# Weight rows in three padded runs, and new planning constants, in a top-k attention and two-MLP kernel

## The chip, the cores and the metric

The kernel runs on one core of a Trainium2 chip. The metric is the device time of one execution in microseconds; the runs of before are 702.24, 703.14 and 704.08 us, median 703.14.

## What is computed

Attention over 2 batches, 8 heads, 576 positions of 64, in which each row keeps its 32 largest scores; the result goes as 1152 tokens of 512 through a leaky MLP of width 2048 and then through a gated product MLP of width 1536.

```python
scores = scale * np.matmul(q, k.transpose(0, 1, 3, 2))
kth = np.partition(scores, -top_k, axis=-1)[..., -top_k:-top_k + 1]
scores = np.where(scores >= kth, scores, -1000000000.0)
attn = np.exp(scores - max); attn = attn / (sum + 1e-09)
x = (attn @ v) as 1152 x 512
...
h = x @ w_in
x = (np.maximum(h, 0.0) + alpha * np.minimum(h, 0.0)) @ w_out
...
return (x @ w_a) * (x @ w_b) @ w_out2
```

The weights are handed in as 64-bit words; in each the kernel finds one 32-bit float spread over a low and a high half.

## The kernel before

**Conversion.** The five weights (wi, wo, wa, wb, w2) are 68 blocks of 128 partitions by 512 words. `to_f32` makes floats of one block: SyncE loads it into a buffer `raw` of six (`RAWB`), ScalarE makes two 16-bit halves of a correction `rlo` (L195, L196), VectorE shifts the high halves left by 3 into the block's place in `wi_sb`, `wo_sb`, `wa_sb`, `wb_sb` or `w2s` (L197: it reads every second 32-bit word), and GpSimd adds the correction in place (L198). After each second block `square` sums its squares on TensorE (L208) and VectorE (L210). w2 is stored to HBM in between and loaded again.

**Attention.** 72 tiles of 128 rows in six groups. `front` makes scores on TensorE (L435), `middle` finds the top 32 on VectorE by four MAX8 (L446, L455) and three MATCH_REPLACE (L453), and forms the masked exponentials (L462); it has eight steps k = 0 to 7. `norm` closes a tile with a reciprocal (L469) and a scaling on GpSimd (L470). `back` transposes: for batch 0 on TensorE at step `KBACK`, for batch 1 ("lifted", the last 36 tiles) by a transposing DMA on SyncE's queue (L488) at step `KLIFT`. `av` multiplies with V (L527, L522). `fetch` runs `FA` tiles ahead.

**The MLPs.** `moe1` and `moe2` run group by group in the order `ORDER`; the first three groups' products take the weights as converted, the later ones as two 16-bit halves that `pair` makes in the background. `l1` and `l3` are matmuls (L610, L614), `l2` and `l4` (L622, L625) add up the outputs. `finish` hands the output of `moe1` to `moe2`: a square sum on ScalarE, three small scale steps on VectorE (`pow2`, L115 to L117), the rescaling into two halves (L695 on ScalarE, L696 on VectorE), transposes (L700) and a copy to `xT` (L701).

**What sets the order.** Three tracks are written out by the loop at the end: `dve` (attention and conversion: 26 blocks mixed with the first eight tiles, then 42 blocks, then the tiles), `mlp`, and `bg` (the pairs). The track whose planned clock plus shift is lowest goes next; `SHIFT_ATT` is taken off the clock of `dve`, `SHIFT_BG` is added to that of `bg`, `T_PAIR` is what a pair is planned at. This gives a priority to each instruction, and at build time a scheduler sets the order on each engine by it; `tc.high_priority(offset=...)` moves the instructions in it ahead, by `HPM` for the activations in the MLPs and by `HPY` for `finish`. On the chip each engine then runs its instructions in that order.

Of the kernel before, what the change touches and what calls it, by code (L numbers as in the profile page):

```python
# [20 lines left out]
B, H, S, D = 2, 8, 576, 64
DM = H * D
# [6 lines left out]
NEG = -3.0e38  # L29

LIFT = 2.0 ** 14
KLIFT = 4
KNORM = 0
KAV = 2
KV = 6
# [2 lines left out]
RLOB = 3  # L38
W2B = 3
# [17 lines left out]
STAGES = [(k, g if isinstance(g, tuple) else (g,)) + NATIVE.get((k, g), (1, 1)) for k, g in ORDER]  # L57
DVE = [('open', 0), ('mix', 26, 8), ('xs', 0), ('conv', 42), ('att', 80)]
RAWB = 6
FA = 5  # L60
QA = 1
VA = 0
GTM = 'mdd'
M2M = 'ppd'
F0 = 1
HPY = 0
HPM = 400
SB = 2
KBACK = 3
KFRONT = 1  # L70
SHIFT_ATT = 2.0
SHIFT_BG = 4.0
T_PAIR = 4.0
T_ATT = 5.8
T_CONV = 1.1
F_PE = 1.1

STEPS = 9
CONV = [(n, i) for i in range(NF1) for n in ("wi", "wo")] + [(n, i) for j in range(0, NF2, 2) for n in ("wa", "wb", "w2") for i in (j, j + 1)]
PASSES = ((0, 0), (0, 1), (1, 0))  # L80
# [6 lines left out]
def tile_topk_attention_moe(ctx: ExitStack, tc: tile.TileContext, qT, kT, vM, vL, wi, wo, al, wa, wb, w2, out):  # L87
# [54 lines left out]
    vpart = small("vpart", 8)  # L142

    def square_v(v, b, hp):
        sq = early.tile([P, DM], I32, tag="rlo", name="vsq", bufs=RLOB).bitcast(BF16)[:, 0:5 * P]
        i = 4 * b + hp
        nc.scalar.activation(sq, v.rearrange("p c n -> p (c n)"), AF.Square, accum_out=vpart[:, i:i + 1])

    def x_scale():
        for hp in range(4):  # L150
            v = early.tile([P, DM], I64, tag="raw", name="v_raw", bufs=RAWB).bitcast(F32)[:, 0:5 * P]
            v = v.rearrange("p (c n) -> p c n", c=5)
            load_v(v, 1, hp)
            square_v(v, 1, hp)
            yield
        big = small("vbig", 2)
        row_max(big[:, 0:1], vpart)
        nc.vector.tensor_scalar(big[:, 1:2], big[:, 0:1], 8.0, None, op0=ALU.mult)
        pow2(big[:, 1:2], vsc[:, 0:1], vsc[:, 1:2], 1)
        sq = early.tile([P, NF1], F32, tag="asq", name="asq", bufs=1)  # L160
        nc.vector.tensor_mul(sq, alpha, alpha)
        row_max(amax, sq)
        nc.vector.tensor_scalar(amax, amax, 1.0, None, op0=ALU.max)
        yield


    wsb, wsc, winv, parts = {}, {}, {}, {}
    for name in ("wi", "wo", "wa", "wb"):
        wsb[name] = cp.tile([P, NBLK[name], DM], F32, tag=f"{name}_sb", name=f"{name}_sb")
    all_parts = small("parts", sum(NPART.values()))  # L170
    k0 = 0
    for name, nb in NBLK.items():
# [5 lines left out]
    w2_st = tc.dram_tile([NF2, P, DM], F32, name="w2_st")  # L178
    w2_pr = tc.dram_tile([NF2, P, 2 * DM], F16, name="w2_pr")

    def w2_tile():
        return sp.tile([P, DM], F32, tag="w2s", name="w2s", bufs=W2B)
    srcs = {"wi": wi, "wo": wo, "wa": wa, "wb": wb, "w2": w2}
    w2_tiles = {}

    def to_f32(dst, name, i):
        raw = early.tile([P, DM], I64, tag="raw", name="raw", bufs=RAWB)
        nc.sync.dma_start(raw, srcs[name][i])  # L190
        lo = raw.bitcast(U32).rearrange("p (n t) -> p n t", t=2)[:, :, 0]
        hi = raw.bitcast(I32).rearrange("p (n t) -> p n t", t=2)[:, :, 1]
        d = dst.bitcast(I32)
        r = early.tile([P, DM], I32, tag="rlo", name="rlo", bufs=RLOB)
        nc.scalar.activation(r.bitcast(I16).rearrange("p (n t) -> p n t", t=2)[:, :, 0], lo, AF.Copy, scale=2.0 ** -29)  # L195
        nc.scalar.activation(r.bitcast(BF16).rearrange("p (n t) -> p n t", t=2)[:, :, 1], hi.bitcast(F32), AF.Sign)  # L196
        nc.vector.tensor_scalar(d, hi, 3, None, op0=ALU.logical_shift_left)  # L197
        nc.gpsimd.tensor_tensor(out=d, in0=d, in1=r, op=ALU.add)  # L198

# [11 lines left out]

    def block(name, i):
        if name == "w2":
            t = w2_tile()
            to_f32(t, name, i)
            nc.sync.dma_start(w2_st[i], t)
            held.append(t)
        else:  # L220
            to_f32(wsb[name][:, i], name, i)
            held.append(wsb[name][:, i])
        if i % 2:
            square(name, i // 2, held[-2:] if name == "w2" else [wsb[name][:, i - 1], wsb[name][:, i]])
# [740 lines left out]
def _layout(inputs):  # L965
    import numpy as np

    c = np.ascontiguousarray
    v = inputs["v"].transpose(0, 2, 1, 3).reshape(B, S, DM)

    def rows(w, n):
        return c(w.reshape(n, P, DM)).view(np.int64)

    def columns(w, n):
        return c(w.reshape(4, P, n, P).transpose(2, 1, 0, 3).reshape(n, P, DM)).view(np.int64)

# [28 lines left out]
```

## Time and profile before

| | before |
|---|---|
| median of 3 runs | 703.14 us |
| span of the profiled execution, first to last instruction | 698.3 us |
| TensorE busy | 611.0 us |
| VectorE busy | 557.5 us |
| ScalarE busy | 482.2 us |
| GpSimd busy | 440.6 us |
| mean granted TensorE clock (1 is full speed) | 0.966 |

The profile is one execution; the time of that execution as a whole isn't given, and the median of the runs lies 4.8 us above its span. Busy times are sums over the span; engines work beside each other, so the sums don't add up to a time. What a stretch is limited by is read from the engine that has no idle time in it, and from what the idle engines wait for.

### The profile page before, as it was taken

The page shows a single profiled execution, that of the slowest core. Times are in us where ns is not written, and L with a number is a line of the kernel's source. Part 1 is how long each engine was busy: PE and PEld are TensorE (multiplying, and loading weights), DVE is VectorE, ACT ScalarE, POOL GpSimd, SP SyncE. Part 2 cuts the span into 40 slices and gives each one's busy share as a digit, 9 for nine tenths or more (in the row PEclk, how much of TensorE's full clock was granted, in tenths as well). Part 3 has the DMA queues.
Part 4 walks back from the last instruction along what each step waited for, and adds up shares of the span by engine and source line. Part 5 has one row for each costly group of instructions (what it writes and reads, how often), then busy time and mean ns, then how long its engine had stood idle before and what let it go on. Part 6 is the DMA issues. An engine that isn't in the chain of part 4 may idle for free.

```text
span 698.3 us, 14902 instructions
## 1 busy us (share of the span) xinstructions
PE 611.0 (87%) x5094; PEld 452.6 (65%) x5094; DVE 557.5 (80%) x1340; ACT 482.2 (69%) x1051; POOL 440.6 (63%) x648
## 2 busy tenths in 40 slices
PE   2465579999999898989968799998899999999997
PEld 1344357678766676767648667765777766677775
DVE  3999999769999979889989879999999998320021
ACT  5886999887889987889878635556656655543232
POOL 5875699886656667879988645655566555223221
PEclk9998668999999999999989999999999999999999
DMA  5996799994420132232287665332245421002243
GB/s 163 313 326 202 249 383 310 322 320 146 126 85 27 35 100 67 88 99 62 59 199 181 185 149 134 93 59 46 63 100 123 129 51 36 18 2 58 64 136 107
DMA packets 98492, 94.57 MB, mean 135 GB/s; under 512 B 50416, under 2 KB 72688, under 8 KB 98416
## 3 DMA queue, kind: packets, MB, share of 16 engines
q1 hardware_dynamic: 97104, 91.26, 45.8%
q10 hardware_dynamic: 1312, 2.36, 0.9%
q8 instruction: 40, 0.66, 0.4%
q14 instruction: 36, 0.29, 0.1%
HBM read 74.33 MB, written 8.65 MB: 119 GB/s over the span
## 4 chain that ended last, share of the span: by engine, by line
PE 53%; DVE 16%; DMA 10%; POOL 7%; issue 6%; ACT 6%; SPq 1%; POOLq 0%; ACTq 0%; DVEq 0%
PE hab L610 12%; PE h L610 9%; PE o L622 7%; PE y L622 6%; DVE wk L453 4%; DMA pt<-e 4%; PE ps L435 4%; DVE m L455 4%; PE o L625 2%; PE ha L614 2%; PE hb L614 2%; PE o L527 2%; PE y L625 2%; DVE e L462 2%; PE o L522 2%
## 5 line engine op out<-in xcount | busy, mean ns | idle before, releaser
L455 DVE MAX8 m<-wk 128x8 f32<-128x576 f32 x216 | 162.6, 753 | 2.5
L601 POOL TENSOR_TENSOR gp<-gt,gp 128x256 f16<-128x256 f32 (+1 forms) x112 | 67.5, 611 | 72.9 <-ACT gp L600 63.9
L453 DVE MATCH_REPLACE8 wk<-m,wk 128x576 f32<-128x576 f32 x144 | 106.8, 742 | 0.0
L610 PE MATMUL h<-xT,wi_sb 128*128 128x256 f16 (+1 forms) x960 | 94.8, 251 | 2.6 <-DVE gt L651 1.6
L610 PEld LDWEIGHTS <-wi_sb 128*128 128x128 f16 x960 | 78.8, 98 | 20.5 <-issue 7.6
L622 PEld LDWEIGHTS <-gp 128*128 128x128 f16 x588 | 54.6, 98 | 57.5 <-issue 6.2
L470 POOL TENSOR_SCALAR e<-e,sm 128x576 f32<-128x576 f32 x72 | 54.2, 753 | 51.8 <-DVE sm L469 47.4
L622 PE MATMUL y<-wo_sb,gp 128*128 128x512 f16 x336 | 82.6, 380 | 1.6 <-POOL gp L601 1.5
L435 PE MATMUL ps<-ks,qh 128*128 128x288 f32 x160 | 48.6, 387 | 28.4 <-DVE e L462 19.3
L610 PE MATMUL hab<-xT,wa_sb 128*128 128x256 f16 (+1 forms) x648 | 66.6, 249 | 3.9 <-ACT xT L701 2.0
L622 PE MATMUL o<-w2s,gp 128*128 128x512 f16 x252 | 63.9, 385 | 2.7 <-DMA w2s<-w_pr 2.5
L610 PE MATMUL hab<-xT,wb_sb 128*128 128x256 f16 (+1 forms) x648 | 66.3, 249 | 0.0
L600 ACT ACTIVATE gp<-gt 128x256 f16<-128x256 f32 (+1 forms) x112 | 42.4, 387 | 33.4 <-DVE gt L783 14.4
L446 DVE MAX8 m<-s 128x8 f32<-128x576 f32 x72 | 54.1, 751 | 12.8 <-ACT s L438 9.4
L610 PEld LDWEIGHTS <-wa_sb 128*128 128x128 f16 x648 | 52.9, 98 | 16.7 <-issue 4.2
L462 DVE SCALAR_TENSOR_TENSOR e<-s,m,ep 128x576 f32<-128x576 f32 x72 | 58.2, 808 | 6.4 <-ACT ep L459 1.5
L783 DVE SCALAR_TENSOR_TENSOR gt<-hab,wb_inv,r 128x256 f32<-128x256 f32 (+1 forms) x36 | 15.6, 434 | 59.6 <-ACT r L777 58.3
L610 PEld LDWEIGHTS <-wb_sb 128*128 128x128 f16 x648 | 52.0, 98 | 5.6 <-issue 0.2
L435 PEld LDWEIGHTS ps<-ks,qh 128*128 128x128 f32 x160 | 29.1, 212 | 40.9 <-DVE e L462 18.4
L459 ACT ACTIVATE ep<-s,nb 128x576 f32<-128x576 f32 x72 | 53.9, 749 | 1.5
L195 ACT ACTIVATE rlo<-raw 128x512 int16<-128x512 uint32 x68 | 53.4, 785 | 2.0 <-DMA raw<-in_wi_dram 1.2
L453 DVE MATCH_REPLACE8 wk<-m,s 128x576 f32<-128x576 f32 x72 | 53.4, 742 | 0.0
(204 smaller groups left out, 1422.6 us busy)
## 6 DMA issues: line engine op xcount, KB each, us to landing
w2s<-w_pr SPq DMA_DIRECT2D x48, 256.0 KB, 2.8
w2s<-w_st SPq DMA_DIRECT2D x36, 256.0 KB, 2.8
raw<-in_wi_dram SPq DMA_DIRECT2D x16, 512.0 KB, 5.4
raw<-in_wo_dram SPq DMA_DIRECT2D x16, 512.0 KB, 6.4
raw<-in_wa_dram SPq DMA_DIRECT2D x12, 512.0 KB, 6.0
raw<-in_wb_dram SPq DMA_DIRECT2D x12, 512.0 KB, 5.8
raw<-in_w_dram SPq DMA_DIRECT2D x12, 512.0 KB, 5.1
kr<-in_kT_dram SPq DMA_DIRECT2D x32, 144.0 KB, 2.9
```

Source lines behind the costliest of these rows:

```text
L195: nc.scalar.activation(r.bitcast(I16).rearrange("p (n t) -> p n t", t=2)[:, :, 0], lo, AF.Copy, scale=2.0 ** -29)
L435: nc.tensor.matmul(ps[:, f, 0:HALF], q[:, h % 2, :], ks[h][:, f * HALF:(f + 1) * HALF], start=i == 0, stop=i == len(mm) - 1)
L446: nc.vector.max(m8[:, 0:8], s)
L453: nc.vector.match_replace(out=wk, in_to_replace=m8[:, 8 * r - 8:8 * r], in_values=src, imm_value=NEG)
L455: nc.vector.max(m8[:, 8 * r:8 * r + 8], wk)
L459: nc.scalar.activation(ep, w2(s), AF.Exp, bias=nb, scale=0.125)
L462: nc.vector.scalar_tensor_tensor(w2(e), w2(s), m8[:, 31:32], ep, op0=ALU.is_ge, op1=ALU.mult, accum_out=sm[:, 0:1])
L470: nc.gpsimd.tensor_scalar(e, e, sm[:, 1:2], LIFT if tl["lift"] else 1.0, op0=ALU.mult, op1=ALU.mult)
L600: nc.scalar.activation(h[:, 0:n], t[:, 0:n], AF.Copy)
L601: nc.gpsimd.tensor_sub(l[:, 0:n], t[:, 0:n], h[:, 0:n])
L610: nc.tensor.matmul(dst[:, 0:n], w[a][:, c * P:(c + 1) * P], x[:, b, c, 0:n], start=k == 0, stop=k == 11)
L622: nc.tensor.matmul(dst, act[b][:, s], w[a], start=i == 0 and k == 0, stop=i == last and k == 2)
```

## The change

On the host each row of 512 words becomes three runs of 171 words (513 with one word of padding), each followed by one word of gap, so a row is 516 words. The buffer `raw` has that shape. The two ScalarE passes and the shift read 3 x 171 words of it; the places that the shift writes are one run of 513, so that each block's last word falls on the first word of the next block, which that block's own shift writes later, or on a word that is added at the end of the weight's buffer. GpSimd's add takes 512 words as before. The planning constants are new.

```diff
-KLIFT = 4
+KLIFT = 6
...
-FA = 5
+FA = 6
...
-HPY = 0
-HPM = 400
+HPY = 400
+HPM = 100
 SB = 2
-KBACK = 3
+KBACK = 2
 KFRONT = 1
-SHIFT_ATT = 2.0
-SHIFT_BG = 4.0
-T_PAIR = 4.0
+SHIFT_ATT = 3.0
+SHIFT_BG = 0.0
+T_PAIR = 5.0
...
+RUN = 171
...
-        wsb[name] = cp.tile([P, NBLK[name], DM], F32, tag=f"{name}_sb", name=f"{name}_sb")
+        wrow[name] = cp.tile([P, NBLK[name] * DM + 1], F32, tag=f"{name}_sb", name=f"{name}_sb")
+        wsb[name] = wrow[name][:, 0:NBLK[name] * DM].rearrange("p (i n) -> p i n", n=DM)
...
     def to_f32(dst, name, i):
-        raw = early.tile([P, DM], I64, tag="raw", name="raw", bufs=RAWB)
+        raw = early.tile([P, 3, RUN + 1], I64, tag="raw", name="raw", bufs=RAWB)
         nc.sync.dma_start(raw, srcs[name][i])
-        lo = raw.bitcast(U32).rearrange("p (n t) -> p n t", t=2)[:, :, 0]
-        hi = raw.bitcast(I32).rearrange("p (n t) -> p n t", t=2)[:, :, 1]
+        lo = raw.bitcast(U32).rearrange("p a (n t) -> p a n t", t=2)[:, :, 0:RUN, 0]
+        hi = raw.bitcast(I32).rearrange("p a (n t) -> p a n t", t=2)[:, :, 0:RUN, 1]
         d = dst.bitcast(I32)
-        r = early.tile([P, DM], I32, tag="rlo", name="rlo", bufs=RLOB)
+        r = early.tile([P, 3 * RUN], I32, tag="rlo", name="rlo", bufs=RLOB)
...
-        nc.vector.tensor_scalar(d, hi, 3, None, op0=ALU.logical_shift_left)
-        nc.gpsimd.tensor_tensor(out=d, in0=d, in1=r, op=ALU.add)
+        nc.vector.tensor_scalar(d.rearrange("p (a n) -> p a n", a=3), hi, 3, None, op0=ALU.logical_shift_left)
+        nc.gpsimd.tensor_tensor(out=d[:, 0:DM], in0=d[:, 0:DM], in1=r[:, 0:DM], op=ALU.add)
...
-            to_f32(wsb[name][:, i], name, i)
+            to_f32(wrow[name][:, i * DM:(i + 1) * DM + 1], name, i)
...
+    def runs(w):
+        w = np.pad(w, ((0, 0), (0, 0), (0, 3 * RUN - DM))).reshape(len(w), P, 3, RUN)
+        return c(np.pad(w, ((0, 0), (0, 0), (0, 0), (0, 1)))).view(np.int64)
```

In the built program the shift's source is 3 runs of 171 and its destination one run of 513; the load is one run of 516 words a partition.

The order on VectorE, from the ninth tile's L462 to its reciprocal, before (`m_860` and `m_1880` are the ninth and tenth tile's maxima in the program's numbering; L115, L137 and L158 are small steps of the scales of V and alpha):

```order
L462 SCALAR_TENSOR_TENSOR e,sm<-s,m_860,ep 128x576
L158 TENSOR_SCALAR vbig<-vbig 128x1
L453 MATCH_REPLACE wk<-m_1880,s 128x576
L210 SCALAR_TENSOR_TENSOR junk,parts<-gram,ident 128x128
L197 TENSOR_SCALAR wo_sb<-raw 128x512
L137 COPY amax<-rmb 128x1
L115 TENSOR_SCALAR e_947<-vbig 128x1
L455 MAX m_1880<-wk 128x8
L197 TENSOR_SCALAR wa_sb<-raw 128x512
L469 RECIPROCAL sm<-sm 128x1
```

The same place in the changed kernel, the last rows up to the ninth reciprocal (its lines are numbered a little higher: L202 is the shift, L468 the masked exponential, L475 the reciprocal; `m_1887` is the tenth tile's):

```order
L202 TENSOR_SCALAR wb_sb<-raw 128x513
L459 MATCH_REPLACE wk<-m_860,wk 128x576
L215 SCALAR_TENSOR_TENSOR junk,parts<-gram,ident 128x128
L202 TENSOR_SCALAR wb_sb<-raw 128x513
L461 MAX m_860<-wk 128x8
L202 TENSOR_SCALAR w2s<-raw 128x513
L468 SCALAR_TENSOR_TENSOR e,sm<-s,m_860,ep 128x576
L459 MATCH_REPLACE wk<-m_1887,s 128x576
L202 TENSOR_SCALAR w2s<-raw 128x513
L461 MAX m_1887<-wk 128x8
L202 TENSOR_SCALAR wa_sb<-raw 128x513
L475 RECIPROCAL sm<-sm 128x1
```

In the piece of before two shifts (the `TENSOR_SCALAR` into `wo_sb`, `wa_sb`) stand ahead of the ninth reciprocal, in that of the changed kernel five; counted from the start 33 against 39 stand ahead of it, at the tenth 40 against 43, at the eleventh 43 against 49, at the twelfth 63 against 64, and all 68 at the fourteenth in both.

The order on VectorE at the changeover from `moe1` to `moe2` of the fourth group, before (`ysq` are the scales, `yb` the rescaled output; the rows into `m_6617` and `m_6738` are attention's):

```order
L117 TENSOR_SCALAR ysq<-e_6868 128x1
L116 TENSOR_SCALAR ysq<-e_6926 128x1
L117 TENSOR_SCALAR ysq<-e_6926 128x1
L446 MAX m_6738<-s 128x8
L453 MATCH_REPLACE wk<-m_6617,wk 128x576
L688 TENSOR_TENSOR ysq<-ysq,back_y 128x1 x2
L696 SCALAR_TENSOR_TENSOR yb<-y_6117,ysq,yb 128x512
L455 MAX m_6617<-wk 128x8
L824 TENSOR_SCALAR u<-ysq 128x1 x2
L696 SCALAR_TENSOR_TENSOR yb<-y_6118,ysq,yb 128x512
```

And in the changed kernel (L116 to L118 are the scale steps, L702 the rescaling):

```order
L117 TENSOR_SCALAR ysq<-e_6868 128x1
L118 TENSOR_SCALAR ysq<-e_6868 128x1
L116 TENSOR_SCALAR e_6932<-ysq 128x1
L461 MAX m_6732<-wk 128x8
L694 TENSOR_TENSOR ysq<-ysq,back_y 128x1
L117 TENSOR_SCALAR ysq<-e_6932 128x1
L118 TENSOR_SCALAR ysq<-e_6932 128x1
L702 SCALAR_TENSOR_TENSOR yb<-y_6118,ysq,yb 128x512
```

Before, two rows of attention (a MAX and a MATCH_REPLACE) stand between the first half's last scale step (the first row) and the first rescaling (L696); now one does (a MAX), between the first half's last scale step (the second row) and the rescaling (L702). The second half's scale steps stand between in both.

## Rows read from the trace of the kernel before

**Rows 1.** The page's slices of VectorE, and the chain by engine.
```profile
DVE  3999999769999979889989879999999998320021
PE 53%; DVE 16%; DMA 10%; POOL 7%; issue 6%; ACT 6%; SPq 1%; POOLq 0%; ACTq 0%; DVEq 0%
```

**Rows 2.** Busy time by stretch (us): PE, PEld, DVE, ACT, POOL, clock, DMA.
```profile
20.00:120.00 100.00, 64.34 (x393) 48.16 (x393) 96.83 (x236) 88.58 (x178) 79.63 (x89) 0.83 0.88 297
120.00:165.00 45.00, 41.62 (x334) 32.43 (x333) 34.69 (x87) 39.10 (x88) 39.51 (x43) 1.00 0.83 281
165.00:340.00 175.00, 165.72 (x1273) 123.20 (x1272) 164.08 (x406) 151.02 (x329) 126.29 (x200) 0.99 0.28 81
340.00:370.00 30.00, 23.66 (x227) 16.68 (x225) 27.04 (x69) 23.68 (x54) 26.48 (x45) 0.89 0.69 169
370.00:480.00 110.00, 102.78 (x888) 75.00 (x886) 99.78 (x224) 64.92 (x143) 65.61 (x101) 0.98 0.52 122
480.00:495.00 15.00, 11.49 (x130) 8.21 (x129) 14.40 (x40) 9.13 (x19) 6.89 (x12) 1.00 0.25 50
495.00:698.00 203.00, 196.80 (x1851) 145.58 (x1849) 111.65 (x264) 95.27 (x227) 84.18 (x143) 1.00 0.30 75
```

**Rows 3.** Line L197: duration in ns, minimum/median/maximum.
```profile
L197 DVE TENSOR_SCALAR wo_sb<-raw x16: 399/767/1419, 21.0 to 93.3; 128x512 int32<-128x512 int32 x16
L197 DVE TENSOR_SCALAR wa_sb<-raw x12: 409/688/1514, 95.0 to 152.4; 128x512 int32<-128x512 int32 x12
```

**Rows 4.** Line L197's busy time and count in two stretches.
```profile
20.00:120.00 100.00, 31.91 (x45) 0.83 0.88 297
120.00:165.00 45.00, 17.88 (x23) 1.00 0.83 281
```

**Rows 5.** Line L198: by group (mean ns after the comma), and minimum/median/maximum.
```profile
L198 POOL TENSOR_TENSOR wo_sb<-wo_sb,rlo 128x512 int32<-128x512 int32 x16 | 20.9, 1306 | 4.5 <-ACT rlo L196 2.1 <-DVE wi_sb L197 1.0 <-DVE wo_sb L197 0.9
L198 POOL TENSOR_TENSOR wo_sb<-wo_sb,rlo x16: 1264/1272/1457, 22.6 to 94.4; 128x512 int32<-128x512 int32 x16
```

**Rows 6.** The page's group of MAX8 over 576 elements.
```profile
L455 DVE MAX8 m<-wk 128x8 f32<-128x576 f32 x216 | 162.6, 753 | 2.5
```

**Rows 7.** The page's loads of wa, and VectorE's waits for loads.
```profile
raw<-in_wa_dram SPq DMA_DIRECT2D x12, 512.0 KB, 6.0
DVE wi_sb L197 <- DMA raw<-in_wi_dram: 4.8, 1, 4.8
```

**Rows 8.** The conversion's two ScalarE passes, by group.
```profile
L195 ACT ACTIVATE rlo<-raw 128x512 int16<-128x512 uint32 x68 | 53.4, 785 | 2.0 <-DMA raw<-in_wi_dram 1.2 <-POOL wa_sb L198 0.5 <-POOL w2s L198 0.3
L196 ACT ACTIVATE rlo<-raw 128x512 bf16<-128x512 f32 x68 | 52.6, 774 | 0.0
```

**Rows 9.** VectorE in time: the eleventh and the twelfth reciprocal.
```profile
114.44 0.14 DVE L469 RECIPROCAL sm<-sm 128x1 f32<-128x1 f32 x1
...
152.31 0.15 DVE L469 RECIPROCAL sm<-sm 128x1 f32<-128x1 f32 x1
```

**Rows 10.** The third changeover in time: VectorE, then TensorE's next layer.
```profile
486.99 0.14 DVE L117 TENSOR_SCALAR ysq<-e 128x1 int32<-128x1 int32 x1
487.05 0.75 DVE L446 MAX8 m<-s 128x8 f32<-128x576 f32 x1
...
487.77 0.74 DVE L453 MATCH_REPLACE8 wk<-m,wk 128x576 f32<-128x576 f32 x1
...
488.57 0.75 DVE L696 SCALAR_TENSOR_TENSOR yb<-y,ysq,yb 128x512 f16<-128x512 f32 x1
...
490.88 0.44 PE L610 MATMUL hab<-xT,wa_sb 128*128 128x128 f16 x5 [1.11 <-ACT xT L701]
```

**Rows 11.** Waits of SyncE's queue and of TensorE on transposes.
```profile
SPq L488 <- ACT e L473: 61.3, 23, 5.0
PE o L522 <- DMA pt<-e: 8.6, 10, 2.1
```

More of the change, by code (lines that the diff above doesn't have):

```diff
@@ L144, in square_v @@
     def square_v(v, b, hp):
-        sq = early.tile([P, DM], I32, tag="rlo", name="vsq", bufs=RLOB).bitcast(BF16)[:, 0:5 * P]
+        sq = early.tile([P, 3 * RUN], I32, tag="rlo", name="vsq", bufs=RLOB).bitcast(BF16)[:, 0:5 * P]
         i = 4 * b + hp
@@ L150, in x_scale @@
         for hp in range(4):
-            v = early.tile([P, DM], I64, tag="raw", name="v_raw", bufs=RAWB).bitcast(F32)[:, 0:5 * P]
+            v = early.tile([P, 3, RUN + 1], I64, tag="raw", name="v_raw", bufs=RAWB).rearrange("p a n -> p (a n)").bitcast(F32)[:, 0:5 * P]
             v = v.rearrange("p (c n) -> p c n", c=5)
@@ L164, in x_scale @@
         yield
-    wsb, wsc, winv, parts = {}, {}, {}, {}
+    wrow, wsb, wsc, winv, parts = {}, {}, {}, {}, {}
     for name in ("wi", "wo", "wa", "wb"):
-        wsb[name] = cp.tile([P, NBLK[name], DM], F32, tag=f"{name}_sb", name=f"{name}_sb")
+        wrow[name] = cp.tile([P, NBLK[name] * DM + 1], F32, tag=f"{name}_sb", name=f"{name}_sb")
+        wsb[name] = wrow[name][:, 0:NBLK[name] * DM].rearrange("p (i n) -> p i n", n=DM)
     all_parts = small("parts", sum(NPART.values()))
@@ L179, in tile_topk_attention_moe, with w2_wide @@
     w2_pr = tc.dram_tile([NF2, P, 2 * DM], F16, name="w2_pr")
+    def w2_wide():
+        return sp.tile([P, DM + 1], F32, tag="w2s", name="w2s", bufs=W2B)
     def w2_tile():
-        return sp.tile([P, DM], F32, tag="w2s", name="w2s", bufs=W2B)
+        return w2_wide()[:, 0:DM]
     srcs = {"wi": wi, "wo": wo, "wa": wa, "wb": wb, "w2": w2}
@@ L188, in to_f32 @@
     def to_f32(dst, name, i):
-        raw = early.tile([P, DM], I64, tag="raw", name="raw", bufs=RAWB)
+        raw = early.tile([P, 3, RUN + 1], I64, tag="raw", name="raw", bufs=RAWB)
         nc.sync.dma_start(raw, srcs[name][i])
-        lo = raw.bitcast(U32).rearrange("p (n t) -> p n t", t=2)[:, :, 0]
-        hi = raw.bitcast(I32).rearrange("p (n t) -> p n t", t=2)[:, :, 1]
+        lo = raw.bitcast(U32).rearrange("p a (n t) -> p a n t", t=2)[:, :, 0:RUN, 0]
+        hi = raw.bitcast(I32).rearrange("p a (n t) -> p a n t", t=2)[:, :, 0:RUN, 1]
         d = dst.bitcast(I32)
-        r = early.tile([P, DM], I32, tag="rlo", name="rlo", bufs=RLOB)
-        nc.scalar.activation(r.bitcast(I16).rearrange("p (n t) -> p n t", t=2)[:, :, 0], lo, AF.Copy, scale=2.0 ** -29)
-        nc.scalar.activation(r.bitcast(BF16).rearrange("p (n t) -> p n t", t=2)[:, :, 1], hi.bitcast(F32), AF.Sign)
-        nc.vector.tensor_scalar(d, hi, 3, None, op0=ALU.logical_shift_left)
-        nc.gpsimd.tensor_tensor(out=d, in0=d, in1=r, op=ALU.add)
+        r = early.tile([P, 3 * RUN], I32, tag="rlo", name="rlo", bufs=RLOB)
+        nc.scalar.activation(r.bitcast(I16).rearrange("p (a n t) -> p a n t", a=3, t=2)[:, :, :, 0], lo, AF.Copy, scale=2.0 ** -29)
+        nc.scalar.activation(r.bitcast(BF16).rearrange("p (a n t) -> p a n t", a=3, t=2)[:, :, :, 1], hi.bitcast(F32), AF.Sign)
+        nc.vector.tensor_scalar(d.rearrange("p (a n) -> p a n", a=3), hi, 3, None, op0=ALU.logical_shift_left)
+        nc.gpsimd.tensor_tensor(out=d[:, 0:DM], in0=d[:, 0:DM], in1=r[:, 0:DM], op=ALU.add)
     def square(name, i, src):
@@ L215, in block @@
         if name == "w2":
-            t = w2_tile()
+            t = w2_wide()
             to_f32(t, name, i)
+            t = t[:, 0:DM]
             nc.sync.dma_start(w2_st[i], t)
@@ L969, in _layout @@
     v = inputs["v"].transpose(0, 2, 1, 3).reshape(B, S, DM)
+    def runs(w):
+        w = np.pad(w, ((0, 0), (0, 0), (0, 3 * RUN - DM))).reshape(len(w), P, 3, RUN)
+        return c(np.pad(w, ((0, 0), (0, 0), (0, 0), (0, 1)))).view(np.int64)
     def rows(w, n):
-        return c(w.reshape(n, P, DM)).view(np.int64)
+        return runs(w.reshape(n, P, DM))
     def columns(w, n):
-        return c(w.reshape(4, P, n, P).transpose(2, 1, 0, 3).reshape(n, P, DM)).view(np.int64)
+        return runs(w.reshape(4, P, n, P).transpose(2, 1, 0, 3).reshape(n, P, DM))
     return {
```

## The prediction

> **What bounds the kernel now.** I read the page's slices and chain first, then the busy time by stretch, then the rows of the lines that the diff touches. The chain that ended last is 53% TensorE and only 16% VectorE [rows 1], but that is a mean over two stages. The stretches separate them [rows 2]: from 20 to 120 us VectorE is busy 96.83 of 100 us and TensorE only 64.34, so attention and the weight conversion on VectorE set the pace. From 120 to 165 us VectorE falls to 34.69 of 45 us while ScalarE has 39.10 and GpSimd 39.51: conversion there waits for those two. From 165 us on TensorE has 165.72 of 175 us, and from 495 us 196.80 of 203 us. So whatever comes earlier on VectorE pays only by closing TensorE's idle time before 495 us: 9.3 us in 165 to 340, 6.3 in 340 to 370, 7.2 in 370 to 480, 3.5 in 480 to 495, together 26.3 us.
>
> **The shift by itself.** One conversion is a load, two ScalarE passes, one VectorE shift (L197) and one GpSimd add. The shift took 399 ns at best and up to 1514 [rows 3]; 45 of them in 20 to 120 us cost 31.91 us (709 ns each), 23 in 120 to 165 us cost 17.88 (777 each) [rows 4]. The add took 1264 ns at best but 1306 in the mean of the wo blocks [rows 5]. The long ones are shifts that wait for an add to end and the other way round. What the shift costs once its source has 3 rows and its destination one run of 513 no row shows. Two rows bound it: 512 elements in 399 ns are 256 steps of two elements, MAX8 reads 576 elements one by one in 753 ns [rows 6]. With one fixed part for both, a step is (753 - 399) / (576 - 256) = 1.11 ns and the fixed part 116; 513 single steps are then 684 ns, and constant if nothing is waited for. Ends: 399 (it stays as it is, and still waits) and 798 (all of the 399 twice). I take 684, the estimate nearest to a row of single steps. In the VectorE-bound stretch that saves 45 x (709 - 684) = **1.1 us**; in the second one 23 x 93 ns = 2.1 us, where VectorE has 10 us idle, so I count 0 there. GpSimd saves some 42 ns an add, 68 x 42 = 2.9 us, of which about half lies in 120 to 165 us; up to 1.5 us would be gained there, and I count none, since ScalarE is as busy.
>
> In the Trainium skill, "Vector Engine (DVE) Microarchitecture Reference", section 5.1, an instruction with one source uses both ports where the outermost counts are even or equal, and the case here (3 against 513, both odd and unequal) is named as not measured. "SBUF — State Buffer", section "Who interferes with whom", has the two-port form exclude GpSimd for a whole instruction; the spread of 399 to 1514 ns agrees.
>
> The other edits of the conversion have one answer. The load grows from 4096 to 4128 bytes a row (0.8%); its median landing time is 6.0 us [rows 7], and VectorE waited for loads only 4.8 us once at the start [rows 7], with six buffers ahead. ScalarE's two passes go from 512 to 513 elements, 785 ns for one pass now [rows 8]. GpSimd's add keeps 512. Zero for all three; if the load's cover went, 0.8% of 6.0 us a block is 0.05 us, 3.3 us over 68 blocks.
>
> **The order: conversions move ahead.** This is the larger term. The order of VectorE shows 43 shifts ahead of the eleventh reciprocal (one closes each attention tile) and 63 ahead of the twelfth; in the changed kernel 49 and 64. In the trace these two stand at 114.44 and 152.31 us [rows 9]: 20 blocks in 37.87 us, 1.89 us a block, of which ScalarE's two passes take 785 + 774 ns [rows 8]. Five blocks fewer in that stretch are 5 x 1.89 = 9.5 us. The six that are moved ahead now stand where VectorE is full: 6 x 0.684 = 4.1 us later at the eleventh tile. Net at the twelfth: -9.5 + 4.1 - 1.1 = **-6.5 us**, to about 146 us. Ends: 0, if ScalarE's work is only moved and not hidden better (it was busy 88.58 of 100 us in the stretch into which it is moved [rows 2], so 11.4 us were free against 6 x 1.56 = 9.4 us needed), and -9.5. What is late next: from 165 us VectorE goes on at attention with the same work, and TensorE at 95%. I let 4 of the 6.5 us through to TensorE's 26.3 us idle: **-4.0 us**, ends 0 and -9.5.
>
> **The changeovers between the two MLP layers.** HPY from 0 to 400 lets the steps that finish a layer's output stand earlier. At the third one VectorE has, in the trace of before, a MAX8 at 487.05 and a MATCH_REPLACE at 487.77 between the last scale step (486.99) and the rescaling of the output (488.57), and TensorE starts the next layer only at 490.88 after 1.11 us of idle [rows 10]. In the new order one attention row, a MAX8, is left between the first half's scale and its rescaling, where two stood: 0.75 us less on that chain, and the rescaling no longer stands behind a MATCH_REPLACE. Three such changeovers have attention beside them; TensorE waits for transposes too [rows 11], so not all of it shows. Estimate **-1.0 us**, ends 0 and -3 (0.75 us at each of the three and one MATCH_REPLACE, 0.74 us, more at one). HPM from 400 to 100 pulls the other way for the activation steps of the MLP; the order shows the same interleaving of weights and outputs in the last 90 us, where TensorE never waits long, so zero, with 2 us kept as its upper end.
>
> KLIFT from 4 to 6 writes the transposing DMA two VectorE steps later (1.5 us). SyncE's queue stood 61.3 us in 23 waits, 2.7 us each, before these DMAs because the data was not ready, and TensorE waited 8.6 us in all for them [rows 11]: a later place costs nothing while the wait is longer than the 1.5 us. Zero, with up to 2 us as its end. KBACK, FA, SHIFT_ATT, SHIFT_BG and T_PAIR act only through the places named; what they move elsewhere in the order are single rows on either side.
>
> **The sum.** -4.0 - 1.0 = -5.0 us on a span of 698.3 us: 693.3. The median of the runs is 703.14, 4.8 us above the span of the profiled execution; that stays. 703.1 - 5.0 = **698.1 us**. The most favourable ends give -9.5 - 3 = -12.5, 690.6 us.
>
> **Rivals.**
> (a) The time gained early is not used: TensorE from 165 us has its own queue, and attention that is ready 6 us earlier finds it busy 95% [rows 2]. For it speaks that the last 203 us hold almost no idle time; against it, that 26.3 us of idle lie before. Only the 1.0 us of the changeovers stays: 702.1 us. Chance 0.17.
> (b) Slower: the conversion is set by ScalarE from 20 us on and not by VectorE. Then six blocks moved ahead delay the tiles before the eleventh by 4.1 us, and the stretch behind gives nothing back, since ScalarE's 39.10 of 45 us [rows 2] are only filled again by what was displaced: 703.1 + 4.1 = 707.2 us. It decides if the twelfth reciprocal stands later than 152.3 us. For it: ScalarE's share in the two stretches, 88.6% and 86.9%. Against: 11.4 us free in the first. Chance 0.14.
> (c) The change does not do what it says: the shift still takes two elements a step and still waits for GpSimd. Durations would spread from 400 to 1500 ns as now; the order alone stays, with six moved shifts at 709 ns, and the waits that it was laid out without come back; I leave half of the 5.0: 700.6 us. Chance 0.07.
> (d) A single-step shift over every second word costs more than a step: any duration between 798 ns and the 1264 of a GpSimd add over 512 elements. At 1.0 us, 45 x (1.0 - 0.709) = 13.1 us more in the VectorE-bound stretch, less the 5.0: 711.2 us. Against it: 399 ns for 512 elements already read every second word without a loss beside MAX8's rate. Chance 0.07. In the Trainium skill, "Vector Engine (DVE) Microarchitecture Reference", section 5.2, a port reaches its full rate only in runs of two adjacent words and pays about 0.65 cycle an element else; by that rule the shift would come near 1 us. The 399 ns speak against it.
>
> **How the numbers follow.** The forecast has 0.55. Faster means below 701.0 and slower above 705.2 (0.3%, about what a measurement of this kernel can tell from no change). The forecast lies below 701.0 with nine tenths of its weight (0.50), (c) with half (0.04), (a) with a quarter (0.04): faster 0.58. Slower: (b) and (d) 0.21, less what of (b) ends within: 0.18. The rest is 0.24. Range: 690.6 by the ends below; above, it must leave out at most a tenth, so it takes in (a) and half of (b): 705.5 us.
>
> **What the changed profile would show.** The shift's rows lie within a few ns of 684 and the adds at 1264: else (c) or (d). The twelfth reciprocal stands near 146 us: else (b). TensorE's idle time between 165 and 495 us falls by some 5 us: else (a). At the third changeover one attention row instead of two stands between the first scale and its rescaling. The prediction is wrong if the tiles come earlier and the end does not, or if new waits show on transposes or on loads.

## The result, and the profile after

| | before | after |
|---|---|---|
| median of the runs, first comparison | 703.46 us (4 runs) | 693.33 us (4 runs) |
| the same, second comparison (`after_again`) | 703.26 us (16 runs) | 694.92 us (4 runs) |
| ratio, first comparison | 1 | 0.9863, 95% interval 0.9832 to 0.9894 |
| ratio, second comparison | 1 | 0.9887, 95% interval 0.9833 to 0.9941 |
| span of the profiled execution | 698.3 us | 694.8 us, second one 690.0 us |
| TensorE busy | 611.0 us | 611.7 us, second one 608.0 us |

The change is worth 8 to 10 us. Each run of after stands 1.8 us above its own span, so its first profiled execution took 696.6 us and is the slowest of its four; the second one took 691.8 us. The rows below are of the first one; where the second differs in a way that matters, its figure is given beside it.

First the same stretches as in [rows 2], of after (columns as there), with the page's chain by engine ahead of them:

```profile
PE 59%; ACT 11%; DMA 10%; DVE 7%; issue 6%; POOL 5%; SPq 1%; POOLq 0%; ACTq 0%; DVEq 0%
...
20.00:120.00 100.00, 69.69 (x454) 52.95 (x455) 94.52 (x242) 94.56 (x196) 83.57 (x97) 0.80 0.93 331
120.00:165.00 45.00, 44.22 (x363) 35.22 (x361) 41.10 (x118) 39.74 (x89) 36.11 (x45) 1.00 0.78 267
165.00:340.00 175.00, 164.80 (x1284) 121.99 (x1283) 166.43 (x403) 154.34 (x339) 133.60 (x213) 0.99 0.29 81
340.00:370.00 30.00, 22.17 (x249) 18.01 (x248) 27.51 (x70) 24.22 (x52) 24.49 (x38) 0.83 0.70 173
370.00:480.00 110.00, 101.30 (x820) 72.05 (x819) 101.60 (x232) 62.37 (x140) 62.77 (x100) 0.98 0.50 110
480.00:495.00 15.00, 14.51 (x156) 13.12 (x155) 14.47 (x34) 9.67 (x19) 6.73 (x11) 0.80 0.41 57
```

Against [rows 2] the gain stands in the first two rows, not where I looked for it. TensorE does 69.69 - 64.34 = 5.35 us more from 20 to 120 us and 44.22 - 41.62 = 2.60 us more from 120 to 165. From 165 to 495 us its idle time, which I had forecast to fall by some 5 us, is 10.2 + 7.8 + 8.7 + 0.5 = 27.2 us against 26.3 before. Behind 495 us it is 6.5 us before and 8.4 us in after. So of TensorE's idle time only the part ahead of 165 us became shorter, from 54.4 to 47.5 us (47.0 in the second execution). VectorE's share of the chain went from 16% [rows 1] to 7% (9% in the second), and in 120 to 165 us its busy time rose from 34.69 to 41.10: with fewer conversions left there, rows of attention fill what was idle.

The shift of after (ns, minimum/median/maximum, as in [rows 3]), and the eleventh and twelfth reciprocal ([rows 9]):

```profile
L202 DVE TENSOR_SCALAR wo_sb<-raw x16: 666/678/683, 22.7 to 85.8; 128x513 int32<-128x513 int32 x16
L202 DVE TENSOR_SCALAR wa_sb<-raw x12: 660/671/690, 87.3 to 140.1; 128x513 int32<-128x513 int32 x12
```

```profile
118.78 0.16 DVE L475 RECIPROCAL sm<-sm 128x1 f32<-128x1 f32 x1
...
140.97 0.16 DVE L475 RECIPROCAL sm<-sm 128x1 f32<-128x1 f32 x1 [0.21 <-ACT sm L469]
```

The shift is constant, near the estimated 684 ns, where it took 399 to 1514 ns before [rows 3]. The eleventh reciprocal stands 4.3 us later than before and the twelfth 11.3 us earlier; I had forecast 6.5 earlier.

Last the waits of TensorE and of SyncE's queue (us in total, times, longest), which answer to [rows 11]; the first line is of before, the others of after:

```profile
PE ps L435 <- DVE e L462: 19.3, 9, 5.6
...
PE ps L441 <- DVE e L468: 10.3, 9, 6.6
...
PE tp L706 <- ACT yb L701: 8.4, 3, 4.4
PE o L528 <- DMA pt<-e: 8.4, 6, 3.2
...
SPq L494 <- ACT e L479: 52.2, 17, 10.5
```

TensorE's wait ahead of new scores, until VectorE has formed masked exponentials, fell from 19.3 to 10.3 us. The wait for the transposing DMAs is as long as before (8.4 against 8.6 us). The wait of its transposes for the rescaled output of an MLP layer (`yb`) is 8.4 us (8.1 in the second execution); before it was 0.9 us.

### The profile page after: what moved, and what is told of

It is laid out like the page before. It is cut to its first block, busy times and chain, and to the rows that moved or that the text cites. A ratio compares the mean times of both kernels' runs of the same rounds, so it can differ in the third digit from the quotient of the medians.

```text
span 694.8 us, 14916 instructions
## 1 busy us (share of the span) xinstructions
PE 611.7 (88%) x5094; PEld 456.1 (66%) x5094; DVE 550.3 (79%) x1340; ACT 480.8 (69%) x1051; POOL 434.2 (62%) x648
## 4 chain that ended last, share of the span: by engine, by line
PE 59%; ACT 11%; DMA 10%; DVE 7%; issue 6%; POOL 5%; SPq 1%; POOLq 0%; ACTq 0%; DVEq 0%
PE hab L616 14%; PE h L616 8%; PE y L628 8%; PE o L628 7%; DMA pt<-e 4%; PE ps L441 4%; PE ha L620 3%; PE o L533 3%; PE hb L620 3%; PE o L631 3%; ACT rlo L200 2%; PE o L528 2%; ACT rlo L201 2%; DVE wk L459 2%; DVE m L461 2%
## 5 line engine op out<-in xcount | busy, mean ns | idle before, releaser
L459 DVE MATCH_REPLACE8 wk<-m,wk 128x576 f32<-128x576 f32 x144 | 107.0, 743 | 0.0
L616 PE MATMUL h<-xT,wi_sb 128*128 128x256 f16 (+1 forms) x960 | 100.0, 257 | 4.4 <-DVE gt L657 2.3
L616 PEld LDWEIGHTS <-wi_sb 128*128 128x128 f16 x960 | 80.3, 100 | 23.8 <-issue 8.3
L616 PE MATMUL hab<-xT,wb_sb 128*128 128x256 f16 (+1 forms) x648 | 68.0, 254 | 0.0
L441 PE MATMUL ps<-ks,qh 128*128 128x288 f32 x160 | 47.1, 379 | 19.4 <-DVE e L468 10.3
L616 PEld LDWEIGHTS <-wa_sb 128*128 128x128 f16 x648 | 54.3, 101 | 15.0 <-issue 2.4
L468 DVE SCALAR_TENSOR_TENSOR e<-s,m,ep 128x576 f32<-128x576 f32 x72 | 58.3, 809 | 4.5 <-PE t L501 1.0
L616 PEld LDWEIGHTS <-wb_sb 128*128 128x128 f16 x648 | 54.2, 101 | 5.9 <-issue 0.2
L200 ACT ACTIVATE rlo<-raw 128x513 int16<-128x513 uint32 x68 | 54.0, 795 | 2.1 <-DMA raw<-in_wi_dram 1.4
L201 ACT ACTIVATE rlo<-raw 128x513 bf16<-128x513 f32 x68 | 53.1, 781 | 0.0
```

The lines of the kernel that those rows point to most:

```text
L200: nc.scalar.activation(r.bitcast(I16).rearrange("p (a n t) -> p a n t", a=3, t=2)[:, :, :, 0], lo, AF.Copy, scale=2.0 ** -29)
L201: nc.scalar.activation(r.bitcast(BF16).rearrange("p (a n t) -> p a n t", a=3, t=2)[:, :, :, 1], hi.bitcast(F32), AF.Sign)
L441: nc.tensor.matmul(ps[:, f, 0:HALF], q[:, h % 2, :], ks[h][:, f * HALF:(f + 1) * HALF], start=i == 0, stop=i == len(mm) - 1)
L459: nc.vector.match_replace(out=wk, in_to_replace=m8[:, 8 * r - 8:8 * r], in_values=src, imm_value=NEG)
L468: nc.vector.scalar_tensor_tensor(w2(e), w2(s), m8[:, 31:32], ep, op0=ALU.is_ge, op1=ALU.mult, accum_out=sm[:, 0:1])
L616: nc.tensor.matmul(dst[:, 0:n], w[a][:, c * P:(c + 1) * P], x[:, b, c, 0:n], start=k == 0, stop=k == 11)
```

## Experiments

**Each half alone.** `layout_only` is the changed kernel with the old constants, `const_only` the kernel before with the new ones.

```diff
 layout_only, against after       const_only, against before
-KLIFT = 6                       -KLIFT = 4
+KLIFT = 4                       +KLIFT = 6
...
```

> The padded rows of 3 x 171 words with the old planning constants. If the gain comes from the shift that takes single steps (port theory: shift and GpSimd add no longer wait for each other), most of it is here: shifts within 657 to 696 ns, adds at 1264 ns, twelfth reciprocal near 141 us, time 693 to 697 us. If it comes from the new constants, the time stays at 702 to 704 us.

> The old rows of 512 words with the new planning constants. Its order has the 68 shifts at the same places among the first 15 tiles as before. Port theory and order theory both expect shifts of 400 to 1500 ns, the twelfth reciprocal near 152 us and 700 to 704 us; the constants theory expects 693 to 696 us.

Measured: `layout_only` 719.01 us, ratio 1.0232 (1.0198 to 1.0266); `const_only` 714.41 us, 1.0168 (1.0143 to 1.0194). Each half alone is slower than before by 11 to 16 us, and both together are faster by 8 to 10. The two effects don't add. In `layout_only` the shifts are constant (679 to 685 ns in the mean of the groups) and the twelfth reciprocal is early, at 147.68 us, and yet the end is late. Its span is 16.6 us longer than that of before: 618.9 - 611.0 = 7.9 us of it is TensorE's busy time for the same 5094 matmuls, 8.7 us is more idle time. Two pieces of 20 us of `layout_only`, then the same of before (columns as in [rows 2]):

```profile
PE 618.9 (87%) x5094; PEld 458.6 (64%) x5094; DVE 552.0 (77%) x1340; ACT 482.8 (68%) x1051; POOL 434.4 (61%) x648
...
280.00:300.00 20.00, 15.36 (x106) 12.37 (x105) 17.50 (x37) 16.38 (x34) 17.73 (x37) 0.98 0.34 101
300.00:320.00 20.00, 18.50 (x144) 13.36 (x144) 19.09 (x45) 17.50 (x39) 15.83 (x31) 0.85 0.30 82
```

```profile
280.00:300.00 20.00, 18.02 (x128) 13.88 (x128) 17.97 (x40) 17.13 (x38) 16.81 (x36) 1.00 0.29 91
300.00:320.00 20.00, 19.01 (x168) 14.20 (x163) 18.23 (x42) 17.10 (x37) 17.32 (x28) 1.00 0.30 84
```

TensorE is busy 15.36 of 20 us in the first piece (before 18.02), and in the next the clock granted to it is 0.85 in the mean, so for a part of it 1.2 instead of 2.4 GHz: 144 matmuls take 18.50 us where before 168 took 19.01. In `const_only` TensorE's busy time is 617.9 us, likewise. So the form does not make the two slow, since one has the new form and the other the old one. What they have in common is a new order, since the scheduler sets it at build time from durations that it assumes, and these change with the shift's form, the priorities with the constants. The next runs were to part form and order.

**Another form of the same layout, with the new constants.** Both kernels are edits of after. `even_runs` has four runs of 128 words with gaps, so that the shift may take two elements a step; `even_mix36` has in addition 36 instead of 26 blocks mixed with the first eight tiles.

```diff
-RUN = 171
+RUN = 128
...
-        raw = early.tile([P, 3, RUN + 1], I64, tag="raw", name="raw", bufs=RAWB)
+        raw = early.tile([P, 4, RUN + 1], I64, tag="raw", name="raw", bufs=RAWB)
...
 even_mix36, besides
-DVE = [('open', 0), ('mix', 26, 8), ('xs', 0), ('conv', 42), ('att', 80)]
+DVE = [('open', 0), ('mix', 36, 8), ('xs', 0), ('conv', 32), ('att', 80)]
```

> New constants, rows stored as four runs of 128 words with gaps: the same gaps and host layout, and the loads again 516 words a row, but the shift's source has 4 runs and its destination 512 words, both even. Port theory: shifts of 400 to 1500 ns as before, twelfth reciprocal near 152 us, 700 to 704 us. If the gaps or the longer load make the gain, it stays at 693 to 696 us. If the scheduler's order alone does, 700 to 704 us, since 43 and 62 shifts stand ahead of the eleventh and twelfth reciprocal.

> As the kernel of four runs of 128, but 36 blocks instead of 26 are mixed with the first eight tiles, so that the order has 45 and 65 shifts ahead of the eleventh and twelfth reciprocal (49 and 64 in the changed kernel). Order theory: the conversions that stand earlier bring the twelfth reciprocal to 141 to 147 us and the time to 693 to 698 us though the shift still waits for GpSimd. Port theory: 1.8 to 1.9 us a block in that stretch as before, twelfth reciprocal at 150 us or later, 700 us or more.

Measured: 715.99 us, 1.0170 (1.0144 to 1.0196), and 715.11 us, 1.0195 (1.0164 to 1.0227). The shift is again spread (means of the groups 672 to 848 and 618 to 992 ns), the twelfth reciprocal at 153.41 and 153.28 us. These two are inconclusive by themselves: their order is again another one.

**A loose order.** `plain_odd` and `plain_even` are after and `even_runs`, built with a scheduler that assumes no durations. On VectorE 1004 of 1020 rows of the two stand in the same place.

```diff
-    with tile.TileContext(nc, schedule_with_timeline_sim=True) as tc:
+    with tile.TileContext(nc, schedule_with_timeline_sim=False) as tc:
```

> The changed kernel (3 runs of 171, new constants) with the build-time scheduler's own timing switched off, so that the order on each engine follows the priorities alone and does not depend on how long a shift is taken to be. To be read beside the kernel of four runs of 128 built in the same way: 1004 of VectorE's 1020 instructions stand at the same place in both. Both will be slower than the changed kernel, some 720 to 800 us. Port theory: this one is 4 to 11 us faster than its partner and its twelfth reciprocal 6 to 13 us earlier. Theory that the port matters nothing to the time: within 3 us of each other.

> The partner: four runs of 128 words, so that the shift takes two elements a step and shares with GpSimd, with the same constants and nearly the same order. Port theory: shifts of 400 to 1500 ns with a mean near 740, 4 to 11 us slower than the partner. Otherwise within 3 us of it.

Measured: 823.84 us, 1.1687 (1.163 to 1.1744), and 821.17 us, 1.1676 (1.1636 to 1.1717). In this order the form is worth nothing that these runs can tell: the twelfth reciprocal stands at 163.62 and 161.70 us, and the two intervals overlap. What a shift costs or saves is read in the order in which it stands, not from its duration.

**The constants in two groups.** `hp_old` takes back `HPY` and `HPM`, `k_old` takes back `KLIFT`, `KBACK` and `FA`.

```diff
 hp_old           k_old
-HPY = 400       -KLIFT = 6
-HPM = 100       -FA = 6
+HPY = 0         -KBACK = 2
+HPM = 400       +KLIFT = 4
                 +FA = 5
                 +KBACK = 3
```

> The changed kernel with the old priorities of the changeover and of the MLP activations (HPY 0, HPM 400). The changed kernel's TensorE waited 8.4 us for the rescaled output, 4.4 us at once, where the prediction had counted a gain. If the new priorities cost at the changeovers, this kernel is 2 to 5 us faster, 688 to 691 us. If the constants only work as a set for one order, it is slower, 695 to 715 us. Twelfth reciprocal near 141 us in any case.

> The changed kernel with the old KLIFT 4, KBACK 3 and FA 5. The layout alone had lost 15 us against the changed kernel after the twelfth tile. If these three carry that, this kernel is at 703 to 719 us; the prediction had them at zero, 692 to 696 us.

Measured: 713.66 us, 1.0140 (1.0097 to 1.0182), and 715.38 us, 1.0154 (1.011 to 1.0198). Either group taken back costs about 20 us against after (both were timed beside before). I had put the first group at -1.0 us and the second at zero. Again the twelfth reciprocal is early (142.72 and 146.09 us) and what is lost is lost behind it: from the twelfth to the 72nd reciprocal 451.0 and 451.2 us, after 436.3 (432.0 in the second execution), before 439.1.

**The form with the order held.** To part order from form, the next kernels change the operands of the finished program, after the scheduler has set the order: each instruction of each engine stays in its place. `pair_form` is after with rows without gaps, so that the passes and the shift read one run of 512 words. `odd_form` and `odd_form2` are the kernel before with a shift of three runs into one of 507.

```diff
 pair_form, against after: for each of the 204 instructions that read raw
-source [[344, 3], [2, 171]], destination [[s, 513]]
+source [[2, 512]],           destination [[s, 512]]
 odd_form2, against before: for each of the 68 shifts; and the adds
-source [[2, 512]],           destination [[1, 512]]
+source [[342, 3], [2, 169]], destination [[1, 507]]
```

> The changed kernel with every instruction of every engine in exactly the same place, and only the form of the conversion changed: the weight rows lie without gaps again (512 words in the same padded row of 4128 bytes), so the shift and ScalarE's two passes read one run of 512. The shift may then take two elements a step. It tells the order from the form. Theory A (the form decides: a two-element shift and a GpSimd add keep each other waiting, and the changed order only works without that): shifts spread from 400 ns upward, adds rise to 1306 ns or more, the twelfth reciprocal falls from 141 to 147-153 us, and the end from 693 to 700-712 us. Theory B (the order decides, the form is worth nothing, as in the pair with the loose order): twelfth reciprocal at 141-143 us, the end at 690-697 us. Theory C (the two-element shift is the better one wherever the order fits, since its best is 399 ns against 676): the end below 690 us.

> The mirror image: the kernel before with every instruction in its place, and only the shift's form changed to single steps: three runs of 169 words, two words apart, into one run of 507. What it leaves out: the last five words of a row are zero and the second and third run are taken two and four words further on, the add covers 507 words, and for the w2 blocks the add subtracts the low part from itself, so w2 is zero; four small fills on GpSimd at the start. Nothing else differs, durations included. Theory A (the form decides): shifts at 668 ns, adds near 1270 ns, block rate between the eleventh and the twelfth reciprocal 1.5-1.7 us instead of 1.89, the twelfth reciprocal at 143-148 us instead of 152, and the end at 694-701 us. Theory B (the order decides): the end within 2 us of the kernel before, twelfth reciprocal at 150-153 us. Theory C (single steps cost more than the waits they save where VectorE is full): the eleventh reciprocal later than 115.5 us and the end slower than before by 2-5 us.

> The changed kernel once more, unaltered, beside the other two on the same chip: the ratio to the kernel before should again lie between 0.983 and 0.990 (691-697 us), the twelfth reciprocal near 141 us, the time from the 72nd reciprocal to the end of the span near 117 us. If the ratio comes out above 0.995, the first comparison was a matter of the chip and not of the kernel.

> odd_form once more, with the w2 blocks treated as all others, since its 12 adds of w2 took 1.04 us instead of 1.32 and so gave GpSimd 3 us that are not the shift's. What it leaves out: the last five words of every row are zero (for w2 by one small fill on GpSimd ahead of each of the 12 adds), the second and third run of a row are taken two and four words further on, the adds cover 507 words. The order is that of the kernel before on every engine. If the form is what counts (theory A): the end 4-7 us faster than before (696-699 us), the twelfth reciprocal at 145-149 us. If odd_form's gain came from its shorter w2 adds (theory D): the end within 2 us of the kernel before, the twelfth reciprocal at 150 us or later.

| order of | shift in pairs | shift in single steps |
|---|---|---|
| before | before: 703.26 us (702.57 beside `odd_form2`) | `odd_form`: 696.92 us, ratio 0.9908 (0.9878 to 0.9937); `odd_form2`: 698.57 us, 0.9936 (0.9911 to 0.9960) |
| after | `pair_form`: 700.17 us, 0.9976 (0.9946 to 1.0006) | `after_again`: 694.92 us, 0.9887 (0.9833 to 0.9941) |

Down a column the order changes, along a row the form. The form is worth 4.0 to 6.3 us in the order of before and 5.2 us in that of after, where the shortest of ten runs of `pair_form` (699.25 us) is longer than the longest of four of `after_again` (698.03 us). The order is worth 3.1 us by the medians with the shift in pairs, which its interval can't tell from nothing, and 2 to 5 us with single steps (696.92 or 698.57 less 694.92 or 693.33), where the runs and the intervals overlap. So the form is shown, and the order's own share is not clear of noise.

Two things bear on the size. `odd_form` has for w2 12 subtractions of 1.04 us in place of adds of 1.27 us, which helps it by up to 3 us; `odd_form2` has 12 fills of 0.1 us that it could do without. And the adds of both cover 507 words instead of 512, by the number of words some 12 ns an add, 0.8 us over 68, as an estimate. The changed values do not show in TensorE's granted clock: 0.944 to 0.965 in the runs of `odd_form2`, 0.946 to 0.970 in those of before beside it.

Shift, add and the two reciprocals of `pair_form`, of the same order as after:

```profile
L202 DVE TENSOR_SCALAR wi_sb<-raw x16: 399/892/1496, 8.2 to 86.7; 128x512 int32<-128x512 int32 x16
L202 DVE TENSOR_SCALAR wa_sb<-raw x12: 405/857/1502, 90.7 to 148.1; 128x512 int32<-128x512 int32 x12
...
L203 POOL TENSOR_TENSOR wa_sb<-wa_sb,rlo 128x512 int32<-128x512 int32 x12 | 16.0, 1331 | 2.0 <-DVE wa_sb L202 1.9
...
124.80 0.16 DVE L475 RECIPROCAL sm<-sm 128x1 f32<-128x1 f32 x1
...
148.55 0.15 DVE L475 RECIPROCAL sm<-sm 128x1 f32<-128x1 f32 x1
```

and of `odd_form2`, of the same order as before:

```profile
L197 DVE TENSOR_SCALAR wo_sb<-raw x16: 649/674/687, 21.7 to 92.3; 128x507 int32<-128x507 int32 x16
L197 DVE TENSOR_SCALAR wa_sb<-raw x12: 649/673/681, 93.7 to 147.6; 128x507 int32<-128x507 int32 x12
...
L198 POOL TENSOR_TENSOR wa_sb<-wa_sb,rlo 128x507 int32<-128x507 int32 x12 | 15.2, 1271 | 0.8 <-PE gram L208 0.6 <-ACT r_n L661 0.2
...
113.00 0.14 DVE L469 RECIPROCAL sm<-sm 128x1 f32<-128x1 f32 x1
...
147.50 0.16 DVE L469 RECIPROCAL sm<-sm 128x1 f32<-128x1 f32 x1 [0.23 <-ACT sm L463]
```

With the order of before, single steps bring the eleventh reciprocal from 114.44 [rows 9] to 113.00 us and the twelfth from 152.31 to 147.50: 1.4 us in the stretch that VectorE fills, and 37.87 - 34.50 = 3.4 us in the one where it has idle time. In this second one GpSimd was busy 34.16 of 37.87 us before and 30.22 of 34.50 in `odd_form2`; its adds alone took 27.05 and 24.42 us, so most of the 3.4 us are adds that no longer wait. With the order of after, pairs make the 68 shifts 55.9 us long in all instead of 45.9, the eleventh reciprocal 6.0 us later and the twelfth 7.6 us later.

How the gain goes on from there to the end is not shown in these two profiled executions: of 4.8 us at the twelfth reciprocal `odd_form2` is 1.0 us ahead at the 72nd and 0.9 us at the end of the span, while that of `odd_form` keeps 5.7, 6.4 and 6.3 us. One execution differs from the next by more than that; the worth at the end rests on the medians of the table.

How it happens shows in time. Two blocks of the kernel before, then two of `odd_form2` (start, duration in us):

```profile
119.70 1.27 POOL L198 TENSOR_TENSOR w2s<-w2s,rlo 128x512 int32<-128x512 int32 x1
119.75 1.51 DVE L197 TENSOR_SCALAR wa_sb<-raw 128x512 int32<-128x512 int32 x1
...
120.94 0.59 POOL L669 TENSOR_TENSOR r_n<-r_n,nalpha 128x128 f32<-128x128 f32 x1
...
121.48 1.28 POOL L198 TENSOR_TENSOR wa_sb<-wa_sb,rlo 128x512 int32<-128x512 int32 x1
...
121.92 1.14 DVE L197 TENSOR_SCALAR wb_sb<-raw 128x512 int32<-128x512 int32 x1
...
123.20 1.28 POOL L198 TENSOR_TENSOR wb_sb<-wb_sb,rlo 128x512 int32<-128x512 int32 x1 [0.43 <-DVE wb_sb L197]
```

```profile
120.20 1.27 POOL L198 TENSOR_TENSOR wa_sb<-wa_sb,rlo 128x507 int32<-128x507 int32 x1
...
121.37 0.67 DVE L197 TENSOR_SCALAR wb_sb<-raw 128x507 int32<-128x507 int32 x1
121.43 1.27 POOL L198 TENSOR_TENSOR wb_sb<-wb_sb,rlo 128x507 int32<-128x507 int32 x1
```

Before, the shift that starts at 119.75 us ends 0.29 us after the add that runs until 120.97, and the next one, from 121.92 us, ends 0.30 us after the add that runs until 122.76; only behind its shift can a block's own add begin. So shifts and adds stand one behind the other, 1.7 to 1.8 us a block here. A small operation of the MLP on GpSimd (L669) stands between the two and is drawn out as well: 577 ns in the median of its eight, 400 in `odd_form2`. In `odd_form2` a shift of 0.67 us runs beside an add and ends in the middle of it, and here the next add follows on the one before.

## Why the prediction was right, and where it was not

The sign, the range and the duration of the shift hold: 693.3 to 694.9 us lie in 690.6 to 705.5. The forecast was about half of the change: -5.0 us forecast, -8 to -10 measured. The way by which the forecast carried the gain to the end was not the one that the trace shows, and two of its own signs of being wrong did show (TensorE's idle time from 165 to 495 us did not fall, and a new wait of its transposes appeared). That the sum came out as near as it did is in part luck. By its own steps:

- **A shift in single steps, 684 ns and constant.** 657 to 696 ns measured. The estimate from MAX8 and the two-element shift was good. Rival (c), that it stays as it was, and rival (d), that it costs 1 us, are out. In the Trainium skill, the page "Vector Engine (DVE) Microarchitecture Reference" names this case (one source, counts odd and unequal) in section 5.1 as not measured; the durations of after fit single steps. The 0.65 cycle an element of its section 5.2 does not show here.
- **1.1 us in the VectorE-bound stretch.** 1.4 us, by `odd_form2`. Right for the order of before, from whose rows it was worked out. In the order of after, with more shifts beside adds, the same change of form is worth 6.0 us up to the eleventh reciprocal (`pair_form`: 124.80 against 118.78 us), and there it was mis-sized.
- **"VectorE has 10 us idle, so I count 0 there", and none for GpSimd's 1.5 us.** This is the step that failed. `odd_form2` gained 3.4 us in just that stretch. I took idle time on each of three engines for slack on each, but a block passes through all three, and shift and add excluded each other: the block time of 1.89 us was not set by ScalarE's 1.56 alone but included 0.17 us of this exclusion. It fell to 34.50 / 20 = 1.73 us with the form alone. In the order of after the same term is 23.75 - 22.19 = 1.6 us, and ScalarE is then busy 21.84 of the 22.19 us.
- **Six blocks moved, -9.5 + 4.1 us, -6.5 us with the shift.** I had reckoned the order with shifts in single steps, which is `odd_form2` against after: +5.8 us at the eleventh (I had 4.1), -12.3 us behind it (I had -9.5), together 140.97 - 147.50 = -6.5 us against my -5.4. Both parts were somewhat too small, and the sign is right. In pairs (`pair_form` against before) the order moved it by +10.4 - 14.1 = -3.8 us, since the shifts up to the eleventh then wait for adds more (818 ns in the mean of 49 shifts, 725 in that of 43 before). At the twelfth reciprocal the whole change is -11.3 us instead of -6.5, and most of what is missing is the form: -4.8 us where I had -1.1.
- **-4.0 us let through, by closing TensorE's idle time from 165 to 495 us.** The end gained more than that by the medians (3.5 us in the first profiled execution, 8.3 in the second), but this idle time did not fall (27.2 against 26.3 us): this step had the wrong path. The work was gained before 165 us: TensorE's idle time there was 54.4 us before and 47.5 in after, and of it the wait ahead of new scores fell from 17.6 to 8.3 us. I had left this stretch out because VectorE set its pace. A part of rival (a) did come true: at the 72nd reciprocal, the last of attention, after is 14.1 us ahead (577.31 against 591.43 us), and from there to the end it takes 117.5 us against 106.9, so 10.6 us are given back. `pair_form` takes 117.4 us there and `odd_form2` 107.0, so that is the order: before had done more of the MLPs ahead of the last tile (TensorE is busy 101.5 us behind it before and 112.3 in after).
- **Changeovers -1.0 us.** Not borne out. At the one near 480 us, which [rows 10] has at 487 us, a single attention row stands between the scale and the rescaling, as forecast, but TensorE's wait for the rescaled output rose from 0.9 to 8.4 us, 3.1 of it there and 5.3 at the changeover ahead of it, near 350 us. In after at the latter:

```profile
349.78 0.58 ACT L691 ACTIVATE yb<-y 128x512 f32<-128x512 f32 x1
...
351.01 0.59 ACT L691 ACTIVATE yb<-y 128x512 f32<-128x512 f32 x1
...
351.58 0.68 ACT L701 ACTIVATE yb<-y,ysq 128x512 f16<-128x512 f32 x1
...
352.32 0.40 PE L706 MATMUL tp<-ident,yb 128*128 128x128 f16 x4 [4.39 <-ACT yb L701]
```

  The two square sums on ScalarE start 1.2 us apart (0.5 before, at 359.2 and 359.7 us), and TensorE's queue has nothing ahead of the transposes that could fill the wait. What the new places cost at the end is not shown: TensorE's idle time as a whole rose by 1.5 us from 340 to 370 us and fell by 3.0 from 480 to 495, where its clock is lower, 0.80 against 1.00.
- **`KLIFT` at zero.** The wait for the transposing DMAs is 8.4 us against 8.6: right as a wait. But "zero" for constants that only place instructions was too bold: `k_old` and `hp_old` show that without them a new order is built, 20 us slower. Such constants carry no term of their own in a sum; they choose the order. `layout_only` too had an early twelfth reciprocal and constant shifts, and it ended at 719 us: the terms that the prediction has for the constants, -1.0 us in all, do not tell the changed kernel from it, so here the prediction had luck.
- **Rival (b), ScalarE sets the pace:** the twelfth reciprocal would be later than 152.3 us. It is at 141 us. Out by that test, though with single steps in the new order ScalarE is the engine that is full from the eleventh to the twelfth (21.84 of 22.19 us).
- **4.8 us between span and median.** After shows 1.8 us between a run and its own span, and in the later comparisons the runs of before stand 1.7 to 1.9 us above theirs. So its profiled execution took about 700.1 us, a quick one. The forecast was not harmed, since the same 4.8 us stood on both sides.

Open: which places make the rebuilt orders 11 to 16 us slower than before. The profile shows that TensorE idles more and then runs at a lower granted clock, not which instruction's place causes it. Why after's order does better than those of `hp_old` and `k_old` was not taken apart further, and neither was how the time gained at the twelfth reciprocal comes to the end.

## What to carry over

Where a block passes from engine to engine, idle time on each is no slack: if two instructions exclude each other, a form with a worse best time (0.67 us instead of 0.40) that runs beside the other one can shorten the block, also where neither engine is quite full. To tell the worth of a form from that of the order that is built around it, hold the order fixed and change the form alone; the orders that this scheduler built here lie some 25 us apart (693 to 719 us). And look for the gain also ahead of the stretch in which the bottleneck engine seems free.

## What the runs showed of the hardware

- A VectorE shift of 513 words in single steps, over every second word, takes 657 to 696 ns whatever GpSimd does, the one of 512 words that may go in pairs 399 to 1514 ns [rows 3]. In the Trainium skill, the page "SBUF — State Buffer", section "Who interferes with whom", has the two-port form exclude GpSimd; the timeline above agrees.
- GpSimd's add lengthens with it: 1331 ns in the mean of the wa blocks in `pair_form`, 1371 in the kernel before, 1289 in after, 1271 over 507 words in `odd_form2`.
- A subtraction on GpSimd whose two sources are the same 512 words took 1039 ns in `odd_form`; the add of two different ones, over 507 words and at the same places, took 1268 ns in `odd_form2`. Whether the operation or the single source makes it shorter no run tells apart.
